# A decode-attention stream: one load cut into 128, 122 and 6 rows, and the last V tiles in fewer loads

## The chip, the core and the metric

The kernel runs on one core of one Trainium2 chip. Its metric is the device time of one launch in microseconds, the median of several runs. A profiled execution of the same program gives, beside its own time, the span from the core's first to its last instruction; every time of an instruction below counts from the start of that span.

## What is computed

One token attends to two caches, and a gate mixes both results. Part A has 16 heads with a cache each; part B has 16 query heads on 8 caches, two to a cache. All caches are 8192 x 256 in float32.

```
def _A_ref(x, k_cache, v_cache, wq, wo):          # H = 16, Dh = 256; B: Hq = 16 on Hkv = 8
    q = (x @ wq).reshape(B, Sq, H, Dh)            # x is 1 x 1 x 448
    scores = jnp.einsum("bhqd,bhkd->bhqk", q, k_cache) * (Dh ** -0.5)
    p = _softmax(scores, axis=-1)
    o = jnp.einsum("bhqk,bhkd->bhqd", p, v_cache)
    return o.reshape(B, Sq, H * Dh) @ wo          # 448 outputs
...
g = _sigmoid((x * gate_w).sum(-1, keepdims=True))
return g * a + (1 - g) * b
```

Each cache element is used for one or two query heads, so nearly all of the 432 MB that the core reads is K and V, read once.

## The kernel before

**One stream.** The host lays everything that is read (x and the gate's weights, Wq, K, V, Wo) into one flat array, in the order of use, and the core reads it from its start to its end. All loads are issued by SyncE on one queue. A buffer (a "slot") has 128 partitions of 15,872 floats (and 16 more), and there are three of them; `plan()` (line 47) cuts the stream into 54 fills of a slot. Most fills are one DMA of 128 rows, one row a partition, 62 KB a row (7936 KB). Within the array a DMA's rows lie one behind the other (line 469).

**Units and tiles.** There are 24 units (8 sets of one head pair of B, r = 2, and two heads of A, r = 0 and 1), each of four tiles of 2048 keys; a K tile or a V tile is 128 x 4096 floats, 2 MB. V runs three tiles behind K (`LEAD`). Each set's Wq stands ahead of its K, its Wo behind.

**The work on a piece** (`piece`, line 416) follows its load in the same order. For K, units with r = 2 and r = 1 take their scores on TensorE (`scores`, line 244, matmul on line 255); those with r = 0 take them on VectorE by row (`scores_by_row`, lines 277 and 281). Minimum, exponential and a transpose follow on VectorE and ScalarE. For V, `attend` (line 307) multiplies by the probabilities on TensorE, 16 rows of 128 keys to a tile, two rows to a matmul. After a unit's last V tile, `take` (lines 316 and 317) and `project_o` (line 372) bring the output into shape; small steps between (`combine`, `column`) are put off by one or two tiles with `wait` and `tick`.

**The order on TensorE** is the program's order: an instruction of a later piece waits behind one of an earlier piece.

**The end.** The last three fills are cut into smaller DMAs so that work can start before a fill is whole: 3072 and 4864 KB; 1280, 2048 and 2048 KB; and the last V tile as `LAST_CUT` = 8, 4 and 4 of its 16 rows (1024, 512 and 512 KB) with the last Wo in four DMAs (448, 448, 672 and 224 KB). In all there are 63 loads. Behind them stand the last `take` and `project_o`, the output matmuls (`emit`, line 398) in two batches of 32, a copy to SBUF (line 483) and the output's DMA, which has four rows of 448 bytes (line 484).

**Waits of the queue.** A fill is issued when its slot's last reader of three fills before is done. Beside that each DMA uses one of eight completion semaphores in turn, so that a load also waits for the landing of the eighth before it.

Of the kernel before, what the change touches and what calls it, by code (L numbers as in the profile page):

```python
# [14 lines left out]
P = 128  # L15
# [19 lines left out]
WQ = (4 * KF + 2) * DH  # L35
UNITS = [2, 0, 1]
BY_ROW = {(s, 0) for s in range(NS)}
LAST_CUT = [8, 4, 4]
HEAD_AT = {2: 0, 0: 2, 1: 3}
TILES = [((s, r), t) for s in range(NS) for r in UNITS for t in range(NT)]  # L40

# [5 lines left out]
def plan():  # L47

    size = {"xg": XG, "k": ROWS * DH, "v": ROWS * DH, "wq": WQ, "wo": 8 * D}
    per = len(UNITS) * NT  # L50
    n = len(TILES)
    items = []
    for i in range(n + LEAD):
        if i == 0:
            items += [("xg", 0), ("wq", 0)]
        if i < n:
            items.append(("k", i))
        if i >= LEAD:
            items.append(("v", i - LEAD))
        if i % per == 7 and i // per + 1 < NS:  # L60
            items.append(("wq", i // per + 1))
        if i % per == LEAD + 1 and i >= per:
            items.append(("wo", i // per - 1))
    loads, room = [[]], FULL
    last = [("v", n - 3), ("v", n - 2)]
    for kind, i in items[:items.index(last[0])]:
        at, left = 0, size[kind]
        while left:
            step = min(left, room) // ATOM[kind] * ATOM[kind]
            if step:  # L70
                loads[-1].append((kind, i, at, step))
            at, left, room = at + step, left - step, room - step * (kind != "xg")
            if left:
                loads.append([])
                room = FULL

    loads = [[x] for x in loads]
    x = loads[-2][0]
    loads[-2] = [x[:2], x[2:]]
    loads[-1] += [[(kind, i, 0, size[kind])] for kind, i in last]  # L80
    at, end = 0, []
    for c in LAST_CUT:
        end.append([("v", n - 1, at, c * DH)])
        at += c * DH

    for h, e, n in ((3, 0, 2), (0, 0, 2), (1, 0, 3), (2, 1, 1)):
        end.append([("wo", NS - 1, (2 * h + e) * D, n * D)])
    return loads + [end]


LOADS = plan()


@with_exitstack
def kernel(
# [5 lines left out]
    nc = tc.nc  # L101
# [314 lines left out]
    def piece(kind, i, at, view):  # L416
        n = view.shape[-1] // ATOM[kind]
        j0 = at // ATOM[kind]
        if kind == "xg":
            inputs(view[:, :KF + 1])  # L420
            GW[0] = view[:, KF + 1:]
        elif kind == "wq":
            project(i, j0, view.rearrange("p (c n) -> p c n", c=n))
            if j0 + n < 2 * KF + 1:
                pass
            elif i == 0:
                spread(0)
                prepare(GW[0])
            else:
                wait(1, spread, i)  # L430
        elif kind == "k":
            u, t = TILES[i]
            if u in BY_ROW:
                scores_by_row(u, t, 2 * j0, view.rearrange("p (j d) -> p j d", d=DH))
            else:
                scores(u, t, j0, view.rearrange("p (c n) -> p c n", c=n))
            if j0 + n < 2 * NG:
                return
            tick()
            if t == NT - 1:  # L440
                gather(u)
                wait(1, combine, u)
                wait(2, column, u)
        elif kind == "v":
            u, t = TILES[i]
            n = view.shape[-1] // DH
            attend(u, t, at // DH, n, view.rearrange("p (j d) -> p j d", d=DH))
            if at // DH + n == ROWS:
                if t == NT - 1:
                    take(u)  # L450
                    if u != TILES[-1][0]:
                        wait(1, project_o, u)
                if i >= len(TILES) - LEAD:
                    tick()
        elif kind == "wo" and i < NS - 1:
            emit_set(i, j0, view.rearrange("p (c n) -> p c n", c=n))
            if i == NS - 2 and j0 + n == 8:
                fold()
        else:
            for j in range(n):  # L460
                LAST[divmod(j0 + j, 2)] = view[:, j * D:(j + 1) * D]

    off = 0
    for fill in LOADS:
        buf = ring.tile([P, FULL + XG], F32, name="slot")
        c = 0
        for load in fill:
            n = sum(x[3] for x in load)
            nc.sync.dma_start(buf[:, c:c + n], stream[off:off + P * n].rearrange("(p n) -> p n", p=P))
            off += P * n  # L470
            for x in load:
                piece(*x[:3], buf[:, c:c + x[3]])
                c += x[3]
# [78 lines left out]
```

## Time and profile before

| | us |
|---|---|
| median of 3 runs | 1010.64 (1010.57 to 1010.64) |
| the profiled execution, its own time | 1010.95 |
| its span | 1009.2 |

| engine | busy us | share of the span |
|---|---|---|
| TensorE matmuls (PE) | 578.0 | 57% |
| VectorE (DVE) | 465.1 | 46% |
| ScalarE (ACT) | 90.0 | 9% |
| DMA queue q1, of 16 engines | | 99.1% |

Mean granted TensorE clock: 0.773 of full speed. The busy share of the DMA engines is a mean over the core's 16 engines. In lines with "out<-in", the first name is what is written; "x16" counts instructions; "[6.31 <-DMA slot]" is idle time before a group and what ended it.

### The profile page before, as it was taken

How to read it: one execution, taken by the hardware profiler on the slowest of the kernel's cores; microseconds unless marked ns; L12 is line 12 of the kernel's file. 1: busy time of each engine (PE TensorE's matmuls, PEld its weight loads, DVE VectorE, ACT ScalarE, POOL GpSimd, SP SyncE). 2: the span in 40 equal slices, each digit the busy share in tenths (PEclk: the TensorE clock that was granted, in tenths of full speed). 3: DMA queues.
4: the chain of work that ended last, by engine and by line, in shares of the span. 5: the costliest groups of instructions: out<-in, count | busy, mean ns of one | idle time of the engine just before them, and what ended most of it. 6: DMA issues, size and time to landing. Idle time of an engine off the chain costs nothing.

```text
span 1009.2 us, 7624 instructions
## 1 busy us (share of the span) xinstructions
PE 578.0 (57%) x3154; PEld 169.8 (17%) x3154; DVE 465.1 (46%) x732; ACT 90.0 (9%) x267; POOL 1.9 (0%) x10
## 2 busy tenths in 40 slices
PE   0846745565745655636646556645656537537557
PEld 0211211121211111112111111111211112111112
DVE  1486213961248521576215841248521585216851
ACT  0100100010100110001100001100110000101010
POOL 0000000000000000000000000000000000000000
PEclk9977877767777887867787777776886777777788
DMA  9999999999999999999999999999999999999997
GB/s 403 439 438 425 431 436 439 435 421 433 439 436 425 436 431 441 431 428 433 441 428 429 438 431 433 435 431 438 431 431 426 440 438 426 428 433 441 424 421 299
DMA packets 9114, 432.50 MB, mean 429 GB/s; under 512 B 1016, under 2 KB 1144, under 8 KB 1784
## 3 DMA queue, kind: packets, MB, share of 16 engines
q1 hardware_dynamic: 9080, 432.02, 99.1%
q8 instruction: 24, 0.39, 0.2%
q14 instruction: 10, 0.08, 0.0%
HBM read 432.02 MB, written 0.00 MB: 428 GB/s over the span
## 4 chain that ended last, share of the span: by engine, by line
DMA 71%; PE 14%; DVE 12%; ACT 2%; issue 1%; ACTq 0%; SPq 0%; DVEq 0%
DMA slot<-in_stream_dram 71%; PE o L307 6%; PE sc L255 5%; DVE sr L281 4%; DVE slot L277 4%; PE sm L220 2%; ACT px L264 1%; DVE mn L261 1%; DVE pr L267 1%; PE sm L237 0%; DVE pr L294 0%; ACT pxr L290 0%; ACT ew L345 0%; PE sm L361 0%; DVE st L262 0%
## 5 line engine op out<-in xcount | busy, mean ns | idle before, releaser
L307 PE MATMUL o<-slot,pr 128*32 128x512 f32 (+1 forms) x1536 | 349.9, 758 | 224.6 <-DMA slot<-in_stream_dram 224.6
L255 PE MATMUL sc<-slot,qb 128*32 128x512 f32 x1024 | 197.5, 715 | 104.7 <-DMA slot<-in_stream_dram 101.7
L261 DVE TENSOR_REDUCE mn<-sc 128x1 f32<-128x512 f32 x64 | 44.1, 690 | 325.7 <-PE sc L255 300.9
L277 DVE TENSOR_TENSOR slot<-slot,qa 128x4096 f32<-128x4096 f32 (+7 forms) x40 | 142.6, 3565 | 41.1 <-DMA slot<-in_stream_dram 41.0
L307 PEld LDWEIGHTS o<-slot,pr 128*32 128x32 f32 (+1 forms) x1536 | 80.0, 142 | 405.2 <-DMA slot<-in_stream_dram 252.8
L281 DVE TENSOR_REDUCE sr<-slot 128x16 f32<-128x4096 f32 (+7 forms) x40 | 142.7, 3567 | 1.4
L255 PEld LDWEIGHTS sc<-slot,qb 128*32 128x32 f32 x1024 | 46.3, 129 | 221.1 <-issue 126.1
L264 ACT ACTIVATE px<-sc,st 128x512 f32<-128x512 f32 x64 | 44.0, 687 | 408.5 <-DVE st L262 386.6
L267 DVE STREAM_TRANSPOSE pr<-px 128x512 f32<-128x512 f32 x64 | 45.6, 713 | 58.9 <-ACT px L264 58.9
L220 PE MATMUL sm<-slot,xz 128*32 128x512 f32 x128 | 45.7, 707 | 35.8 <-DVE xz L193 23.0
L290 ACT ACTIVATE pxr<-sr,st 128x16 f32<-128x16 f32 x32 | 9.8, 308 | 373.6 <-DVE st L288 373.6
L372 PE MATMUL sm<-sel,ob 128*128 128x1 f32 (+1 forms) x96 | 17.5, 287 | 37.3 <-DVE ob L317 37.3
L317 DVE SCALAR_TENSOR_TENSOR ob<-o,half,ob 128x256 f32<-128x256 f32 x24 | 11.3, 470 | 44.0 <-ACT ob L316 44.0
L372 PEld LDWEIGHTS sm<-sel,ob 128*128 128x128 f32 x96 | 15.5, 228 | 61.8 <-DVE ob L317 53.6
L220 PEld LDWEIGHTS sm<-slot,xz 128*32 128x32 f32 x128 | 11.1, 128 | 65.4 <-issue 27.8
L294 DVE TENSOR_TENSOR pr<-pxr,cols 128x256 f32<-128x256 f32 x32 | 13.6, 426 | 15.9 <-ACT pxr L290 15.9
L316 ACT ACTIVATE ob<-o,half 128x256 f32<-128x256 f32 x24 | 11.3, 469 | 49.5 <-PE o L307 49.5
L361 PE MATMUL sm<-ones,wr 1*128 1x1 f32 x48 | 9.7, 268 | 10.4 <-DVE wr L354 10.4
L237 PE MATMUL sm<-px,spread 64*128 64x256 f32 x16 | 6.6, 498 | 13.9 <-DVE es L347 13.9
L381 PE MATMUL Y<-slot,ocs 128*1 128x448 f32 x112 | 13.4, 595 | 0.0
L361 PEld LDWEIGHTS sm<-ones,wr 1*128 1x128 f32 x48 | 7.8, 203 | 32.8 <-issue 28.1
L264 ACT ACTIVATION_READ_ACCUMULATOR px<-sc,st 128x1 f32 x64 | 12.3, 193 | 0.0
(73 smaller groups left out, 142.4 us busy)
## 6 DMA issues: line engine op xcount, KB each, us to landing
slot<-in_stream_dram SPq DMA_DIRECT2D x50, 7936.0 KB, 42.6
slot<-in_stream_dram SPq DMA_DIRECT2D x1, 7940.0 KB, 22.0
slot<-in_stream_dram SPq DMA_DIRECT2D x1, 4864.0 KB, 41.0
slot<-in_stream_dram SPq DMA_DIRECT2D x2, 2048.0 KB, 25.3
slot<-in_stream_dram SPq DMA_DIRECT2D x1, 3072.0 KB, 29.9
slot<-in_stream_dram SPq DMA_DIRECT2D x1, 1280.0 KB, 20.8
slot<-in_stream_dram SPq DMA_DIRECT2D x1, 1024.0 KB, 24.2
slot<-in_stream_dram SPq DMA_DIRECT2D x2, 512.0 KB, 25.5
```

The source lines that it names most:

```text
L220: nc.tensor.matmul(q[BLK * a:BLK * (a + 1), :], xz[:, c if c < KF else KF + a, :], w[:, j, :], start=(c == 0), stop=(c == KF), skip_group_ ...
L255: nc.tensor.matmul(sc[32 * g:32 * (g + 1), :], qb[:, e, at:at + 32], kt[:, j, :], start=(e == 0), stop=(e == 1), skip_group_check=True)
L261: nc.vector.tensor_reduce(mn, sc, axis=AX.X, op=OP.min)
L264: nc.scalar.activation(px, sc, AF.Exp, bias=st[:, 0, t:t + 1], scale=-1.0, accum_out=st[:, 1, t:t + 1])
L267: nc.vector.transpose(pr.rearrange("p (q r k) -> p q k r", r=BLK, k=2), px.rearrange("p (q k c) -> p q k c", c=BLK, k=2))
L277: nc.vector.tensor_tensor(kt, kt, QA[u][:, None, :].to_broadcast([P, n, DH]), op=OP.mult)
L281: nc.vector.tensor_reduce(sc[:, j0:j0 + n], kt, axis=AX.X, op=OP.add)
L294: nc.vector.tensor_tensor(pr, px[:, :, None, :].to_broadcast([P, ROWS // 2, NG * NT, 2]), cols[:, t].rearrange("p g r -> p (g r)")[:, None ...
L307: nc.tensor.matmul(O[u][w * g:w * (g + 1), :], pr[:, j // 2, :w], vt[:, j - j0:j - j0 + 2, :], start=(t == 0 and j < 2 * P // w), stop=(t ...
L361: nc.tensor.matmul(cl, WR.pop(u).rearrange("p c x m k -> p (c x m k)"), ones[:1, :], start=True, stop=True)
L372: nc.tensor.matmul(oc[:, e, :M], OB[u][:, e::2], SEL[u][:, :M], start=True, stop=True)
L381: nc.tensor.matmul(YY[0][32 * h:32 * h + 1, :], OC[s, r][:, e, m:m + 1], wt[:, j, :], start=False, stop=(s == NS - 2 and e == 1), skip_gro ...
```

## The change

The second fill (the fill with number 1) goes as three DMAs: its 128 rows without their last 512 columns, then these 512 columns (2 KB a row) of rows 0 to 121 as one DMA and of rows 122 to 127 as another. Where the bytes go is unchanged. At the end, the fill of 3072 + 4864 KB is one DMA of 7936 KB; the piece of 1280 KB and the whole tile behind it go as one of 3328 KB; the last V tile is cut in 8 and 8 rows. There are 62 loads.

```diff
@@ -35,7 +35,10 @@
-LAST_CUT = [8, 4, 4]
+SKEW = 1
+SKEW_ROWS = 122
+SKEW_N = 512
+LAST_CUT = [8, 8]
@@ -75,9 +78,9 @@
     loads = [[x] for x in loads]
-    x = loads[-2][0]
-    loads[-2] = [x[:2], x[2:]]
-    loads[-1] += [[(kind, i, 0, size[kind])] for kind, i in last]
+    v1, v2 = [(kind, i, 0, size[kind]) for kind, i in last]
+    loads[-1][0].append(v1)
+    loads[-1].append([v2])
@@ -461,12 +464,17 @@
-    for fill in LOADS:
+    for f, fill in enumerate(LOADS):
         buf = ring.tile([P, FULL + XG], F32, name="slot")
         c = 0
         for load in fill:
             n = sum(x[3] for x in load)
-            nc.sync.dma_start(buf[:, c:c + n], stream[off:off + P * n].rearrange("(p n) -> p n", p=P))
+            rows = stream[off:off + P * n].rearrange("(p n) -> p n", p=P)
+            parts = [(0, P, 0, n)]
+            if f == SKEW:
+                parts = [(0, P, 0, n - SKEW_N), (0, SKEW_ROWS, n - SKEW_N, n), (SKEW_ROWS, P, n - SKEW_N, n)]
+            for p0, p1, n0, n1 in parts:
+                nc.sync.dma_start(buf[p0:p1, c + n0:c + n1], rows[p0:p1, n0:n1])
             off += P * n
```

## Rows read from the trace of the kernel before

**Rows 1.** The page: DMA engines' busy tenths in 40 slices of the span.

```profile
DMA  9999999999999999999999999999999999999997
```

**Rows 2.** The page: the chain that ended last, shares of the span by engine.

```profile
DMA 71%; PE 14%; DVE 12%; ACT 2%; issue 1%; ACTq 0%; SPq 0%; DVEq 0%
```

**Rows 3.** The chain of waits, its end: start us, us, what.

```profile
985.98 18.74 DMA slot<-in_stream_dram
...
1004.76 1.58 PE Y L398 x32
...
1006.37 0.27 DVE ys L483
```

**Rows 4.** Windows: us, busy of PE, PEld, DVE, ACT, POOL, PEclk, DMA share, GB/s.

```profile
920.00:960.00 40.00, 20.94 (x89) 6.03 (x89) 32.82 (x32) 2.52 (x10) 0.00 (x0) 0.75 1.00 433
...
996.00:998.00 2.00, 2.00 (x18) 0.55 (x10) 0.00 (x0) 0.00 (x0) 0.00 (x0) 1.00 1.00 405
998.00:999.00 1.00, 0.73 (x9) 0.16 (x8) 0.16 (x1) 0.00 (x0) 0.00 (x0) 1.00 0.99 396
999.00:1000.00 1.00, 0.78 (x6) 0.14 (x4) 0.00 (x0) 0.00 (x0) 0.00 (x0) 1.00 0.77 305
1000.00:1001.00 1.00, 0.80 (x6) 0.14 (x4) 0.00 (x0) 0.00 (x0) 0.00 (x0) 1.00 0.64 252
1001.00:1002.00 1.00, 0.91 (x4) 0.00 (x0) 0.00 (x0) 0.00 (x0) 0.00 (x0) 1.00 0.60 237
1002.00:1003.00 1.00, 0.00 (x0) 0.00 (x0) 0.48 (x1) 0.47 (x1) 0.00 (x0) 1.00 0.55 224
1003.00:1004.00 1.00, 0.94 (x20) 0.90 (x24) 0.17 (x2) 0.00 (x0) 0.00 (x0) 1.00 0.48 186
1004.00:1005.00 1.00, 0.81 (x36) 0.54 (x32) 0.00 (x0) 0.00 (x0) 0.00 (x0) 0.97 0.12 45
```

**Rows 5.** The page: DMA queue, kind: packets, MB, share of 16 engines.

```profile
q1 hardware_dynamic: 9080, 432.02, 99.1%
q8 instruction: 24, 0.39, 0.2%
q14 instruction: 10, 0.08, 0.0%
```

**Rows 6.** DMA packets of the window 1006:1009.2, which holds the output's DMA alone.

```profile
DMA packets 8, 0.00 MB, mean 1 GB/s; under 512 B 8, under 2 KB 8, under 8 KB 8
```

**Rows 7.** The page: DMA issues, KB each, us from issue to landing.

```profile
slot<-in_stream_dram SPq DMA_DIRECT2D x50, 7936.0 KB, 42.6
```

**Rows 8.** Waits of SyncE's DMA queue: us in total, times, longest.

```profile
SPq L469 <- DVE sr L281: 478.3, 24, 25.7
SPq L469 <- PE o L307: 158.2, 15, 16.6
SPq L469 <- DMA slot<-in_stream_dram: 152.5, 25, 10.9
```

**Rows 9.** Timeline of the end, some matmul groups: start us, us, instruction, count.

```profile
974.72 1.90 PE L255 MATMUL sc<-slot,qb 128*32 128x512 f32 x16
...
982.93 3.64 PE L307 MATMUL o<-slot,pr 128*32 128x512 f32 x16 [6.31 <-DMA slot<-in_stream_dram]
...
995.82 1.92 PE L307 MATMUL o<-slot,pr 128*32 128x512 f32 x16 [2.65 <-DMA slot<-in_stream_dram]
...
998.32 1.06 PE L307 MATMUL o<-slot,pr 128*32 128x512 f32 x8 [0.27 <-DMA slot<-in_stream_dram]
...
1000.86 1.05 PE L307 MATMUL o<-slot,pr 128*32 128x512 f32 x4 [0.20 <-DMA slot<-in_stream_dram]
...
1003.62 0.95 PE L398 MATMUL Y<-slot,ocs 128*1 128x112 f32 x32
...
1004.76 1.55 PE L398 MATMUL Y<-slot,ocs 128*1 128x112 f32 x32 [0.19 <-DMA slot<-in_stream_dram]
```

**Rows 10.** Windows of PE alone: us, busy of PE, PEclk, DMA share, GB/s.

```profile
982.90:989.00 6.10, 6.07 (x33) 0.59 1.01 429
```

## The prediction

> **What bounds the kernel now.** I read the slices of the DMA engines first: they are busy at 9 tenths or more in all slices but the last [rows 1]. The chain that ended last is DMA for 71% of the span [rows 2]; its other parts are work that released a slot while older loads still ran. So the transfers bound it: 432.02 MB on sixteen engines that are busy 99.1% of the span [rows 5]. The question is then whether an engine ever runs dry. SyncE does wait for readers of a slot, 478.3 and 158.2 us in all [rows 8], but a load of 7936 KB takes 7936 KB / 433 GB/s = 18.8 us [rows 4] and lands 42.6 us after its issue [rows 7]: some 23.8 us of older transfers lie ahead of each load when it is issued. The engines don't run dry, and a share of 1.00 from 920 to 960 us says the same [rows 4].
>
> The windows of the last microseconds then show what sets the end [rows 4]. All sixteen engines are busy up to 999 us; the share falls to 0.64 and 0.60 by 1002, stands at 0.55 from 1002 to 1003 and ends at 0.12. A share of 0.56 is nine of sixteen: some seven engines finish near 999 to 1000.5, the nine others at 1003 to 1004.8. Each of those nine still runs at full speed (224 GB/s over 8.8 engines is 25.5 a piece). Each DMA of 128 rows gives each engine eight rows, so the shares of data were equal, and the late engines lost their 4 to 5 us by something else. 34 instruction packets [rows 5] are the candidate. The chain ends with the last loads until 1004.72, 32 output matmuls of 1.58 us and the copy [rows 3].
>
> **What the change does, part by part.** The sum is made against the profiled execution, span 1009.2 and own time 1010.95, which is 0.31 above the median of 1010.64; I subtract from that median in the end.
>
> *Bytes of the second load.* The last 512 columns are 2 KB a row. At 433 GB/s / 16 = 27.1 GB/s an engine needs 0.0757 us for 2 KB [rows 4], so an engine that now moves eight such rows spends 0.605 us on them. Small rows cost more: from 996 to 998 us, with rows of 3.5 to 4 KB, all engines are busy but move 405 GB/s [rows 4]; 3.9 KB then takes 0.154 instead of 0.144 us, 0.010 us for each row, so 2 KB takes 0.086. Where the 128 pieces land decides all. The number of engines of a DMA is not always sixteen: 9080 packets [rows 5] are 63 x (128 + 16) + 8, one completion for each engine of a load, and the output's four rows made 8 packets [rows 6], four rows and four completions, so four engines. For 122 rows this trace has no case. The bounds: spread as now, 0; taken off most engines and put on few, -0.6 us for those relieved, and for a busy one, if two share 122 rows, 61 rows and one of the six: 62 x 0.086 - 0.605 = +4.7 us. (One engine alone would be given 128 x 0.086 - 0.6 = +10.4; I keep that as the far end and give it almost nothing.) I take the concentrated case on engines of the early lot, -0.6 for the end: the only row count here that isn't 128 used fewer than sixteen engines.
>
> [...]
>
> *Does the early lot have the room?* An early engine ends at about 999.5, so it would end at 999.5 + 4.7 = 1004.2, against 1004.8 - 0.6 = 1004.2 for the last of the late ones. It just fits. What covers the extra transfer is the idle 5 us at the end, nowhere else; the engine runs 4.7 us behind from the second load on, and loads 2 and later land up to that much later. The readers then free slots later, still within the 23.8 us of queued work [rows 7]; if that cover were gone the queue would idle by the difference.
>
> *Two more issues at the start, one fewer in all.* The added issues stand on SyncE before the third load, which has two loads, 37.6 us of transfers, ahead of it: nothing. The turn of the eight semaphores shifts by two, and each load then waits for an older landing; such waits are 152.5 us in 25 cases now [rows 8], all under queued transfers, and stay so.
>
> *Three fewer loads at the end.* Each engine handles 24 fewer rows of the small-row kind: 24 x 0.010 = 0.24 us less on all engines, ahead of the last V rows. [...]
>
> *Later work on TensorE.* The K tile whose scores ran at 974.72 now lands with the whole fill, where TensorE's wait ended at 982.93 less 0.8, near 982. So these scores, 16 matmuls in 1.90 us at full clock [rows 9], and the half V tile ahead of it, 8 of some 1 us, move behind 982. [...]
>
> *Coarser last cut.* Eight rows take 1.06 us, four took 1.05 [rows 9]: +0.01. The last V rows land where they did, and from there to the first batch of output matmuls the gap stays; this batch ends 0.19 us before the load that the second batch waits for [rows 9], so a delay over 0.2 us counts in full. The second batch took 1.55 against 0.95 us for the first [rows 9], so the clock fell within it; other idle times ahead may bring 0.6 either way. I take 0, as in the row.
>
> Sum: -0.6 - 0.24 + 0.01 = -0.83: own time 1010.95 - 0.8 = 1010.1, and median 1010.64 - 0.8 = 1009.8; with 0.05 for what the fit of the early lot may cost, 1009.9.
>
> **The rivals.**
>
> *R1, a busy engine is a late one (slower).* One mechanism: if 122 rows go to two engines and one of these is among the nine late ones, that one ends the run. Price +4.7 - 0.24 = +4.5, less that engine's own lead over the last. The nine end on average (0.48 + 0.12) x 16 / 9 = 1.1 us after 1003, 0.7 before the last [rows 4]: +3.8, 1014.4 (1013.7 to 1015.1). It decides as soon as the engine's lead is under about 4 us. For it: nine of sixteen are late, and no row names them. [...]
>
> *R2, nothing is concentrated (the skew doesn't take place).* 122 rows spread over sixteen engines: only the fewer small rows are left, -0.24: 1010.4.
>
> [...]
>
> *R4, all sixteen end together.* The engine time idle from 998 to 1005 is 0.01 + 0.23 + 0.36 + 0.40 + 0.45 + 0.52 + 0.88 = 2.85 us [rows 4], so no shift of bytes can gain more than 2.9 + 0.24: 1007.5 to 1008.5. Two engines alone can't level nine; nearly excluded.
>
> **How the numbers follow.** That few engines take the 122 rows I hold at 0.65 to 0.7, and that these are early ones at 0.6, a judgement and the weakest step here. Forecast 0.39; R1 0.27; R2 0.25; R3 0.06; R4 0.03. The forecast's own range is 1009.2 to 1010.5. The whole reaches from 1009.2, through R2 and R3, to the middle of R1: 1014.4; what is left out is R4 and half of R1, some 0.17. A difference of 0.2%, 2 us, is about what a measurement of this kernel can tell from none. Faster by more: R4 alone, 0.04. Within: the forecast, R2 and R3, 0.68. Slower: R1 and a little else, 0.28.
>
> **What would show it.** Packets on q1: sixty loads of 144, the output's 8 and the six rows' 12 give 8660; with 122 + 2 for the skewed DMA 8784, with 122 + 16 it is 8798. If the early lot took the bytes, the windows of the last 5 us stand at a share nearer to 0.7 than to 0.55 until the end, and the last load lands near 1003.9 in the span. If R1 holds, a long stretch at 0.06 or 0.12 stands at the end. If TensorE is late, the second half of the last V tile shows no wait for its load. The forecast is wrong if the span's end moves by over 2 us either way.

## The result, and the profile after

The changed kernel takes 1014.34 us (median of five, 1013.71 to 1014.93), the kernel before 1010.57 (1010.53 to 1010.64) on the same chip: a ratio of 1.0036, 95% interval 1.0025 to 1.0047. That is 3.8 us slower, where I forecast 0.7 us faster and gave "slower" 0.28. The profiled execution has its own time 1013.84 and its span 1012.1, both 2.9 us above those of before, so the traces can account for 2.9 of the 3.8.

The page first, each line for itself: DMA tenths in 40 slices, the queues' packets, the shares of the chain.

```profile
DMA  9999999999999999999999999999999999999996
...
q1 hardware_dynamic: 8784, 432.02, 99.0%
...
DMA 74%; PE 12%; DVE 12%; ACT 1%; issue 1%; SPq 0%; ACTq 0%; DVEq 0%
```

Against [rows 1, 2, 5] nothing large has changed: transfers bound it still, and DMA's part of the chain grew by three points. The count of packets is exact and answers the first open question: 8784 is the figure for 122 rows on two engines (and 6 rows on six).

The end of the chain (start us, us, what) shows where the 2.9 us stand.

```profile
979.61 28.52 DMA slot<-in_stream_dram
...
1008.17 0.99 PE Y L401 x32
...
1009.19 0.28 DVE ys L491
```

The tail of TensorE's timeline (the same columns; in brackets the idle time before) stands beside [rows 9].

```profile
986.48 1.94 PE L310 MATMUL o<-slot,pr 128*32 128x512 f32 x8 [8.73 <-DMA slot<-in_stream_dram]
988.19 3.64 PE L258 MATMUL sc<-slot,qb 128*32 128x512 f32 x16
...
1001.78 1.06 PE L310 MATMUL o<-slot,pr 128*32 128x512 f32 x8
1004.25 1.07 PE L310 MATMUL o<-slot,pr 128*32 128x512 f32 x8 [1.40 <-DMA slot<-in_stream_dram]
...
1007.05 0.95 PE L401 MATMUL Y<-slot,ocs 128*1 128x112 f32 x32
1008.17 0.95 PE L401 MATMUL Y<-slot,ocs 128*1 128x112 f32 x32 [0.17 <-DMA slot<-in_stream_dram]
```

Against [rows 3]: the last load but one (672 KB) releases the last output matmuls at 1008.17 instead of 1004.76, 3.41 us later; these take 0.99 instead of 1.58; the copy starts 2.82 later. So the last transfers are late by 3.4 us, and TensorE gives 0.6 back. TensorE itself isn't the bound: the second half of the last V tile still waited 1.40 us for its load.

Windows of the last microseconds (us, busy of PE, PEld, DVE, ACT, POOL, PEclk, DMA share, GB/s) tell who is late.

```profile
1003.00:1004.00 1.00, 0.00 (x0) 0.00 (x0) 0.00 (x0) 0.00 (x0) 0.00 (x0) 1.00 0.71 287
1004.00:1005.00 1.00, 0.75 (x8) 0.16 (x8) 0.00 (x0) 0.00 (x0) 0.00 (x0) 1.00 0.66 262
1005.00:1006.00 1.00, 0.31 (x4) 0.00 (x0) 0.05 (x1) 0.47 (x1) 0.00 (x0) 1.00 0.27 104
1006.00:1007.00 1.00, 0.51 (x4) 0.51 (x4) 0.43 (x1) 0.00 (x0) 0.00 (x0) 1.00 0.08 32
1007.00:1008.00 1.00, 1.00 (x34) 0.69 (x33) 0.16 (x1) 0.00 (x0) 0.00 (x0) 1.00 0.06 25
1008.00:1009.00 1.00, 0.83 (x32) 0.60 (x32) 0.00 (x0) 0.00 (x0) 0.00 (x0) 1.00 0.01 5
```

Up to 1005 the share is 0.66 to 0.71, eleven engines of sixteen where [rows 4] had nine: two early engines have joined the late ones, as forecast. But then 0.08 and 0.06 stand for two microseconds: 1/16 is 0.0625, so *one* engine runs alone, at 25 GB/s, about what each of the nine has in [rows 4] (224 GB/s over 0.55 x 16 = 8.8 engines, 25.5). It sets the end.

The records of the last load's sixteen completions, sorted, say it by engine (us after the first of them; the first itself in the second column):

```
kernel              first    the other fifteen
before              999.58   0.0 0.1 0.1 0.7 0.7 | 1.9 | 4.5 4.6 4.7 4.7 4.8 4.9 5.1 5.6 5.7
after              1000.82   0.1 0.1 0.7 1.0 | 4.6 4.6 4.6 4.7 4.8 5.0 5.1 5.3 5.5 5.9 | 7.9
```

Two engines left the early lot: one that stood near 0, and the one at 1.9. The completions of every load, read in turn, show how. When the third fill's load lands, two engines stand 5.4 and 5.6 us behind the first, where before the last of all was 1.5 behind. One of the two is still 5.3 behind at the end; the other loses another 1.0, 0.7 and 0.7 on the way and is the one at 7.9. And the first engine itself is 1.24 later, though it was to be relieved.

The same reading shows when the nine engines of the kernel before fell behind: at the instruction packets, which the prediction named as a candidate. From one load to the next the distances between the engines hardly move (their sum by 0.4 us at most), except around such a packet. Around one of 16 KB a single engine falls back by about 1.55 us (from 1.16 to 2.72 between the loads at 115 and 134 us, with a packet at 127.7), around one of 8 KB by 0.7 to 1.0. With 24 and 10 of them [rows 5], the sum of the sixteen distances grows from 5.3 us at the second load to 48.1 at the last.

### The profile page after: what moved, and what is told of

The parts are those of the page before. It is cut to its first block, busy times and chain, and to the rows that moved or that the text cites. A ratio compares the mean times of both kernels' runs of the same rounds, so it can differ in the third digit from the quotient of the medians.

```text
span 1012.1 us, 7626 instructions
## 1 busy us (share of the span) xinstructions
PE 576.6 (57%) x3154; PEld 168.1 (17%) x3154; DVE 465.0 (46%) x732; ACT 90.2 (9%) x267; POOL 1.9 (0%) x10
## 3 DMA queue, kind: packets, MB, share of 16 engines
q1 hardware_dynamic: 8784, 432.02, 99.0%
## 4 chain that ended last, share of the span: by engine, by line
DMA 74%; PE 12%; DVE 12%; ACT 1%; issue 1%; SPq 0%; ACTq 0%; DVEq 0%
DMA slot<-in_stream_dram 74%; PE o L310 6%; PE sc L258 5%; DVE sr L284 5%; DVE slot L280 5%; ACT px L267 1%; DVE mn L264 1%; DVE pr L270 0%; PE sm L223 0%; ACT ew L348 0%; SPq L477 0%; DVE pr L297 0%; ACT pxr L293 0%; PE sm L364 0%; PE sm L240 0%
## 5 line engine op out<-in xcount | busy, mean ns | idle before, releaser
L310 PE MATMUL o<-slot,pr 128*32 128x512 f32 (+1 forms) x1536 | 346.4, 747 | 228.1 <-DMA slot<-in_stream_dram 227.9
L258 PE MATMUL sc<-slot,qb 128*32 128x512 f32 x1024 | 202.9, 734 | 106.0 <-DMA slot<-in_stream_dram 105.8
```

The source lines that it names most:

```text
L258: nc.tensor.matmul(sc[32 * g:32 * (g + 1), :], qb[:, e, at:at + 32], kt[:, j, :], start=(e == 0), stop=(e == 1), skip_group_check=True)
L310: nc.tensor.matmul(O[u][w * g:w * (g + 1), :], pr[:, j // 2, :w], vt[:, j - j0:j - j0 + 2, :], start=(t == 0 and j < 2 * P // w), stop=(t ...
```

## The experiments

Medians in us; "before" is the kernel before on the same chip; the interval is that of the ratio.

| run | this | before | ratio, 95% |
|---|---|---|---|
| skew_only | 1013.93 | 1010.69 | 1.0030, 1.0018 to 1.0041 |
| tail_only | 1011.88 | 1010.69 | 1.0008, 0.9999 to 1.0017 |
| split16 | 1011.49 | 1010.69 | 1.0007, 0.9999 to 1.0016 |
| probe (one run) | 1018.13 | 1010.69 | |
| tail_merge | 1010.71 | 1010.64 | 1.0002, 0.9993 to 1.0011 |
| tail_cut | 1011.39 | 1010.64 | 1.0008, 0.9999 to 1.0017 |
| skew_dense | 1013.70 | 1010.64 | 1.0029, 1.0018 to 1.0041 |
| skew_big | 1018.11 | 1010.64 | 1.0072, 1.0059 to 1.0084 |
| skew_256 | 1011.14 | 1010.70 | 1.0004, 0.9995 to 1.0013 |
| rowshift | 1031.87 | 1010.70 | 1.0210, 1.0196 to 1.0224 |
| warm | 1010.57 | 1010.70 | 0.9998, 0.9989 to 1.0007 |
| split128 | 1010.82 | 1010.64 | 1.0001, 0.9992 to 1.0010 |

The ratio is an estimate of its own and needn't be the quotient of the two medians: for tail_only that would be 1.0012.

### Which half of the change costs?

*skew_only* is the kernel before with the second load cut as in the change:

```diff
+            rows = stream[off:off + P * n].rearrange("(p n) -> p n", p=P)
+            parts = [(0, P, 0, n)]
+            if f == 1:
+                parts = [(0, P, 0, n - 512)] + [(a, b, n - 512, n) for a, b in ((0, 122), (122, P))]
+            for p0, p1, n0, n1 in parts:
+                nc.sync.dma_start(buf[p0:p1, c + n0:c + n1], rows[p0:p1, n0:n1])
```

> The three DMAs of the second load with the old cut of the last loads. Theory: 1014.5, the whole of the loss and 0.2 more. Rival (the tail costs): near 1010 to 1011. In the trace the windows from 39 to 46 us should show whether all engines lose time there, some 2 us, or only those that hold the 122 rows.

*tail_only* is the changed kernel with the second load whole:

```diff
-            if f == SKEW:
+            if False:
```

> The second load as in the kernel before, only the last loads cut as in the changed kernel. If the skewed DMAs alone cost the 3.8 us (theory), this is at 1010.3, 0.2 below the kernel before, by 24 fewer small rows an engine. If the later K tile makes TensorE late at the end (rival), it is at 1011 to 1014 and the last V half has no wait for its load.

The skew alone costs 3.2 us. The tail alone costs 1.2 in the median, where a gain of 0.2 was expected, with an interval that just holds 1. The skew carries the result. The two would add to 4.4, not to 3.8; a possible reason stands under "The tail".

### Which engines are they?

*probe* adds, after fill 40, seven small DMAs of 1 to 7 rows, and a GpSimd memset of each one's tile, which has to wait for its landing; after fill 48 the same with 8 to 15 rows.

```diff
+        if f in (40, 48):
+            for k in range(1, 8) if f == 40 else range(8, 16):
+                pb = const.tile([16, 64], F32, name=f"pb{k}")
+                nc.sync.dma_start(pb[:k, :], stream[:k * 64].rearrange("(p n) -> p n", p=k))
+                nc.gpsimd.memset(pb[:k, :], 0.0)
```

No trace numbers the engines. In the expectations, here and below, engine 0 is the one that a DMA of one row runs on, engine 1 the one that a DMA of two rows has beside it, and so on. That each further row adds an engine to those before, and that the 122 rows ran on 0 and 1, is my assumption.

> The kernel before, with tiny DMAs of 1 to 7 rows behind fill 40 and of 8 to 15 rows behind fill 48; GpSimd overwrites each one's tile, so the start of its memset is the landing. If a DMA of k rows runs on the first k engines, the landing of k rows is that of the latest of these k. Theory: engine 0 early, and 1 early by 4 us or less, so that the start steps up by 1 to 2 us at two rows at most and by 3 to 5 us at some later count. Rival (engine 0 or 1 is of the nine late ones): the start at 1 or 2 rows is already 4 us behind the first engines. If the rows are spread in another way all starts agree. Its time is not of interest: some us over the kernel before.

The timeline of GpSimd in that run (start us, us, what, idle time before; the pause it puts into the stream makes the run 7.4 us slower):

```profile
771.23 0.14 POOL L478 MEMSET pb<- 1x64 f32 x1 [767.82 <-DMA pb<-in_stream_dram]
772.60 0.32 POOL L478 MEMSET pb<- 2x64 f32 x2 [1.23 <-DMA pb<-in_stream_dram]
776.17 0.68 POOL L478 MEMSET pb<- 4x64 f32 x4 [3.25 <-DMA pb<-in_stream_dram]
```

The DMA of one row is done at 771.23, those of two and three rows at 772.60, that of four at 776.17. The fifteen DMAs add 9320 - 9080 = 240 packets to q1, their 120 rows and 120 completions, as many as k engines for k rows give. The one-row DMA lands 0.18 us after the first completion of the load ahead of it (771.00), the two-row DMA 0.18 after one that is 1.38 behind that. I read each landing as that of the latest engine of its DMA: engine 0 is early, engine 1 is 1.4 us behind it, engine 2 no later than that, engine 3 some 5 us behind. If the 122 rows ran on engines 0 and 1, both are early ones, and engine 1 fits the lone 1.9 in the table of completions. That naming is assumed; the landings and the distances are measured. The table tells the same without names, since it is the early lot that lost two: R1's condition, that one of them is among the nine, doesn't hold. In the changed kernel the DMA of 122 rows has two completions, at 47.06 and 47.44 us, and that of 6 rows has six, four of them by 40.32 and two at 47.28 and 47.63, each some 0.2 behind one of the two, so I take the two busy engines to be among those six.

The eight memsets behind fill 48 run without a further wait from 930.04 on and order nothing. The first pause had let the engines draw level: at the next load the last is 1.9 us behind the first, not over 5 as ahead of the pause. An engine's lateness is thus gathered in the run and doesn't belong to the engine.

### How far does the cost follow the bytes?

*skew_256* moves 256 columns instead of 512 in the same way (122 and 6 rows).

```diff
+                parts = [(0, P, 0, n - 256)] + [(a, b, n - 256, n) for a, b in ((0, 122), (122, P))]
```

> As skew_only with 256 columns, 1 KB a row. Engine 1 then carries some 2.6 us more than the others instead of 5.3; with its own 2.0 it stays ahead of the late engines, so they set the end. If the others' loss goes with the bytes that two engines write alone, it is 1 us, less 0.3 us of relief: +0.7, 1011.4. If the others' loss goes with the number of short rows (61 an engine, as before) it stays at 2 us: 1012.4. If the loss came only from engine 1 ending last, there is none: 1010.4.

*skew_big* takes 1024 columns, as 64, 62 and 2 rows: an engine of the busy two gets 4 + 31 + 1 = 36 short rows, not 62, each twice as long. (q1 has 9228 packets, 80 + 64 + 4 more than before: sixteen, two and two engines. That the two are the same ones each time is assumed.)

```diff
+                parts = [(0, P, 0, n - 1024)] + [(a, b, n - 1024, n) for a, b in ((0, 64), (64, 126), (126, P))]
```

> The last 1024 columns of the second load as 64, 62 and 2 rows: engines 0 and 1 carry 28 rows of 4 KB more than in the kernel before, about the same bytes as 54 of 2 KB, in half as many pieces; the others have four rows of 4 KB less (the same 16 KB). If the others' loss goes with the number of short rows it halves to 1 us: 1012.5 to 1013. If it goes with the bytes or with the time that two engines work alone: 1013.9.

Half the bytes cost 0.4 us, within the interval; twice the bytes 7.5, more than either case of its expectation. So it isn't a price for each row: with 36 for 62 on the two engines skew_big costs more than twice as much.

*split128* cuts the second load in the same place but sends the 512 columns as one DMA of 128 rows; *split16* sends them as 112 and 16 rows, each DMA on sixteen engines (q1 has 9240 packets, (112 + 16) + (16 + 16) more than before).

```diff
+                parts = [(0, P, 0, n - 512), (0, P, n - 512, n)]                                                    # split128
+                parts = [(0, P, 0, n - 512)] + [(a, b, n - 512, n) for a, b in ((0, 112), (112, P))]                # split16
```

Theory A in the expectations assumes that a DMA of 128 rows pairs each engine with the same partitions every time; no trace names an engine or a partition.

> [...] If the pairing of engine and partition is what slows the engines (theory A), nothing is lost beyond the cost of eight more rows, 0.1 us: 1010.7, and the windows behind the second load are those of the kernel before. If short rows in the stream cost by themselves, some 0.5 us as in split16: 1011.2 or more.

> As skew_only, but the last 512 columns go as 112 and 16 rows, so that both counts divide by 16 and every engine has eight short rows as others have; same three DMAs, same bytes, same short rows. Theory (the concentration on two engines costs): 1010.7, the kernel before and 0.1 for eight more rows an engine. Rival (short rows or two more DMAs in the stream cost by themselves): 1012.6, with 2 us lost by all engines behind the second load.

split128 costs nothing, so 128 short rows and an additional DMA are free in this place. By the counts split16 has the same bytes on each engine as split128, and is 0.8 us above its before; the interval begins at 0.9999, but all eleven runs are at 1011.16 or more.

The trace records each DMA packet with its start and duration. From 15 to 90 us these records give the duration of a piece, in ns, mean and median:

```
kernel       short rows           62-KB rows begun 38:42  42:46  46:50 (means)
before       none                              2346   2362   2360
split128     2 KB:  84,  84                    2338   2362   2358
split16      2 KB:  99,  84                    2779   2372   2372
skew_256     1 KB:  60,  61                    2778   2494   2366
skew_dense   2 KB: 122, 132                    3122   3098   2445
after        2 KB: 121, 131                    2933   3119   2462
skew_big     4 KB: 292, 294                    4175   4074   3314
```

This is the centre of the case. In a DMA of 128 rows a 2-KB piece takes 84 ns, as the prediction's 0.086 says; with 122 and 6 rows it takes 121 in the mean (131 in the median). And the other engines' own rows, of the next loads, take up to 3.4 us instead of 2.34 while the short rows run. Windows show the same (columns as above). First the kernel before:

```profile
39.00:46.00 7.00, 4.43 (x22) 1.16 (x24) 3.01 (x6) 1.44 (x5) 0.00 (x0) 0.76 1.01 437
46.00:60.00 14.00, 6.51 (x30) 1.82 (x26) 11.98 (x18) 1.11 (x6) 0.00 (x0) 0.86 1.00 432
...
20.00:60.00 40.00, 25.77 (x131) 7.29 (x131) 18.32 (x37) 5.07 (x15) 0.00 (x0) 0.91 1.00 432
```

The kernel after:

```profile
39.00:46.00 7.00, 4.68 (x34) 1.52 (x32) 3.79 (x9) 2.09 (x6) 0.00 (x0) 1.00 1.15 372
46.00:60.00 14.00, 4.71 (x22) 1.18 (x18) 11.19 (x17) 0.82 (x4) 0.00 (x0) 0.76 0.93 397
...
20.00:60.00 40.00, 24.31 (x131) 7.06 (x131) 18.32 (x37) 5.07 (x15) 0.00 (x0) 0.91 0.99 402
```

And skew_big:

```profile
20.00:60.00 40.00, 24.72 (x131) 6.99 (x131) 18.31 (x37) 5.07 (x15) 0.00 (x0) 0.88 0.99 372
```

The share stays near 1 on the whole while the GB/s fall: the engines are busy, and slow. Whole packets are put down to one window, sixteen of 62 KB at a time, so a short window can be off by some per cent. The clean measure is the completion of the last load's first engine: 999.58 before, 999.75 split128, 1000.08 split16, 1000.09 skew_256, 1001.07 skew_only, 1001.08 skew_dense, 1003.82 skew_big. The fourteen engines that were to gain from the skew lose from it, 1.5 us with 512 columns, 0.5 with 256, 4.2 with 1024.

### What slows the rows?

Three causes were open: the short rows' distance in DRAM (62 KB from one to the next), their being short, and theory A, that an engine writes to other partitions than in a DMA of 128 rows. *skew_dense* lays the 128 pieces one behind the other in the array and keeps the two DMAs:

```diff
+    (q, i, at, w) = loads[1][0][-1]
+    loads[1] = [loads[1][0][:-1] + [(q, i, at, w - 512)], [(q, i, at + w - 512, 512)]]
...
+            for p0, p1 in ((0, 122), (122, P)) if n == 512 else ((0, P),):
+                nc.sync.dma_start(buf[p0:p1, c:c + n], rows[p0:p1])
```

> As skew_only, but the host lays the 128 pieces of 2 KB one behind the other, so that the DMAs of 122 and 6 rows read an unbroken stretch and not 2 KB at every 62 KB. If the pitch of the source made the other engines lose 2 us, they lose little here and the run is near 1012 (engine 1's own 5 us are left: +1.3). If what counts is that two engines write single short rows to all partitions, it stays at 1013.9 and the windows from 20 to 60 us move as little as in skew_only.

3.1 us, as skew_only's 3.2, with the pieces at 122 ns in the mean. The short rows' distance in DRAM is not it.

*rowshift* sends the whole second load, rows of 62 KB, as DMAs of 112 and 16 rows. All sixteen engines take part (the packets are below), by that count with eight rows each as before, seven and one, and nothing is short; only how the rows are dealt out is changed.

```diff
+            for p0, p1 in ((0, 112), (112, P)) if f == 1 else ((0, P),):
+                nc.sync.dma_start(buf[p0:p1, c:c + n], rows[p0:p1])
```

> [...] If writing to partitions that otherwise belong to another engine is what slows all engines (theory A), this load takes 4 to 7 us longer: 1014 to 1018. If it is the work of two engines alone (theory B), it costs next to nothing: 1010.8.

It costs 21.2 us, more than the load itself takes (18.8) and than the 4 to 7 of theory A. Its windows (columns as above):

```profile
20.00:60.00 40.00, 13.65 (x83) 4.10 (x83) 5.49 (x17) 3.48 (x9) 0.00 (x0) 0.75 1.01 224
60.00:80.00 20.00, 11.99 (x48) 3.14 (x48) 12.46 (x19) 1.61 (x6) 0.00 (x0) 0.76 0.96 411
```

And its page's line of q1 (packets, MB, share):

```profile
q1 hardware_dynamic: 9096, 432.02, 99.1%
```

9096 is 62 x 144 + (112 + 16) + (16 + 16) + 8: both DMAs ran on sixteen engines. They stay busy at 224 GB/s, half the rate. In the packet records the 62-KB rows of the 112 take 2.9 to 4.8 us, 4.2 in the mean, instead of 2.34, those of the 16 rows up to 8.6. So neither short rows nor few engines are needed. What all slow cases share, and split128 and before don't, is that an engine's rows aren't the eight of a DMA of 128 rows. Whether it is the writes to SBUF that meet, or the reads of other rows in DRAM at the same time, rowshift doesn't separate.

Theory B, next to no cost, is out. Theory A had a fifth to a third of the 21.2 us, and that engines meet at the partitions they write was not shown. In rowshift the first sixteen of the 112 rows all take 3.9 to 4.5 us, so the slowing is there from the first rows. In the skew the fourteen engines had 0.6 us of relief forecast, and they lost 1.5. Both amounts stay open.

### The tail

*tail_cut* is the kernel before with only the coarser last cut; *tail_merge* is tail_only with the old cut.

```diff
-LAST_CUT = [8, 4, 4]
+LAST_CUT = [8, 8]       # tail_cut; tail_merge puts [8, 4, 4] back into tail_only
```

> Only the last cut changed to 8 and 8, everything else as before. Theory: 1011.5 to 1012, TensorE idle over 1 us before the last V half and the clock at 0.5 in the last microseconds of at least the profiled run or of most runs. Rival: 1010.7, as the kernel before.

> The merged fills near the end with the last V tile still cut 8, 4, 4; the second load as before. Theory (the coarse last cut lets TensorE idle 1.4 us ahead of the last half, its granted clock falls and the output matmuls run at the lower level): 1010.4, with the clock at 1.0 up to 1004 us. Rival (the merged fills, which move a K tile's work, upset the clock): near tail_only, 1011.5 to 1012.

tail_merge is the kernel before (+0.07 us): fewer loads bring nothing that can be measured. tail_cut's runs reach from 1010.46 to 1012.75, tail_merge's from 1010.25 to 1011.78, before's from 1010.26 to 1011.24. By their intervals none differs from before; the median and the spread point to the cut, but don't secure it. The traces show what can happen. TensorE's timeline in tail_only:

```profile
998.25 1.07 PE L310 MATMUL o<-slot,pr 128*32 128x512 f32 x8 [0.21 <-DMA slot<-in_stream_dram]
1000.73 1.83 PE L310 MATMUL o<-slot,pr 128*32 128x512 f32 x8 [1.42 <-DMA slot<-in_stream_dram]
1003.71 1.01 PE L375 MATMUL sm<-sel,ob 128*128 128x1 f32 x4 [1.15 <-DVE ob L320]
1004.65 3.17 PE L401 MATMUL Y<-slot,ocs 128*1 128x112 f32 x64
```

Windows of the same run (columns as above):

```profile
1000.00:1002.00 2.00, 1.27 (x8) 0.16 (x8) 0.00 (x0) 0.00 (x0) 0.00 (x0) 0.72 0.61 240
1002.00:1004.00 2.00, 0.85 (x6) 0.29 (x2) 0.48 (x1) 0.47 (x1) 0.00 (x0) 0.50 0.49 194
```

TensorE's timeline in tail_merge:

```profile
1000.85 1.05 PE L310 MATMUL o<-slot,pr 128*32 128x512 f32 x4 [0.17 <-DMA slot<-in_stream_dram]
1003.06 0.63 PE L375 MATMUL sm<-sel,ob 128*128 128x1 f32 x4 [1.16 <-DVE ob L320]
1003.62 0.95 PE L401 MATMUL Y<-slot,ocs 128*1 128x112 f32 x32
1004.77 0.95 PE L401 MATMUL Y<-slot,ocs 128*1 128x112 f32 x32 [0.20 <-DMA slot<-in_stream_dram]
```

And in tail_cut:

```profile
1001.15 1.07 PE L307 MATMUL o<-slot,pr 128*32 128x512 f32 x8 [1.42 <-DMA slot<-in_stream_dram]
...
1005.06 1.64 PE L398 MATMUL Y<-slot,ocs 128*1 128x112 f32 x32 [0.17 <-DMA slot<-in_stream_dram]
```

With 8 and 8 rows TensorE idles 1.42 us ahead of the last half, with 8, 4 and 4 never over 0.3 ahead of a piece of that tile. In tail_only's profile the granted clock then fell, to 0.72 in the mean of 1000 to 1002 and 0.50 from 1002 on: the last V rows take 1.83 instead of 1.07, the 64 output matmuls 3.17. They end at 1007.82 instead of 1005.72, though the last transfer landed at 1005.15 against 1005.30. In tail_cut's profile, after the same 1.42, the clock was 1.00 until 1004, 0.79 in the mean of 1004 to 1006 and 0.50 behind that: the first batch took 0.95 us, the last 1.64. In the changed kernel it stayed at 1.00 to the end after an idle time of 1.40. From 996 to 1000 TensorE had been busy for 3.10 us in tail_only, 3.30 in tail_cut and all 4 in the changed kernel. So nearly the same idle time had three outcomes, and what decides among them stays open. In the changed kernel's profile the tail's cut cost nothing, which may be why the two halves don't add. The kernel before had a fall as well, in its last batch [rows 9], to a clock of 0.50 from 1005 to 1006.

*warm* puts 16 matmuls of zeros, which add nothing to the output, into the idle time ahead of the last `project_o` of tail_merge:

```diff
+    for _ in range(16):
+        nc.tensor.matmul(YY[0][:, :YN], zero, zero[:, :YN], start=False, stop=False, skip_group_check=True)
```

> tail_merge (last cut 8, 4, 4) with sixteen matmuls of zeros, 112 columns each, added to the output behind the last V matmuls, where TensorE waits 1.2 us for the last output to be brought into shape. If the clock at the end is what spreads the runs, more of them stay at the higher level and the median is 0.3 to 0.6 below tail_merge, 1010.2; if these matmuls are not enough to hold it, as tail_merge, 1010.7; if they delay the last product, 0.3 above.

1010.57 against 1010.70, no difference. No version here beats the kernel before.

## Why the prediction was wrong

**"Does the early lot have the room?" is the step that failed.** Concentration, two engines, both early: that much held. "An early engine ends at about 999.5 ... It just fits" gave both engines the lead of the first one, and a price of 4.7 us. The measured terms:

- *The price.* The piece was mis-sized, 0.086 us for 0.121 in the mean: 62 x 0.121 - 0.605 = +6.9, not +4.7. The row it came from [rows 4] was of 128-row DMAs, where 84 ns is right. The engine at 1.9 goes from 1001.5 to 1008.2 in skew_only (+6.7), to 1008.5 in skew_dense (+7.0) and to 1008.7 in the changed kernel (+7.2). The last is 0.5 above the sum less 0.24 for the merged loads; one of its instruction packets cost that engine 1.0 where the others cost 0.7. In skew_256 the same sum, 62 x 0.060 - 0.30 = +3.4, puts it at 1004.9, under the last one's 1005.7, and the time hardly moves.
- *The room.* That engine's lead over the last is 5.7 - 1.9 = 3.8 us, not 5.3 (the first engine's is 5.7). I read "some seven engines near 999 to 1000.5" off the shares as one lot; one of them wasn't. With the forecast's own price it would have ended 4.7 - 0.24 - 3.8 = 0.7 us after before's last one: no gain, and still no loss over 2 us. The price is the larger error: 7.2 for 4.7 - 0.24 = 4.5, so 2.7 us, against 5.3 - 3.8 = 1.5 of lead.
- Together: 7.2 - 3.8 = +3.4 at the last transfer, which is the +3.41 of the chain.

**"Bytes of the second load", the -0.6 for the relieved engines,** had the wrong sign: they lost 1.5 us (first completion +1.24 after -0.24 for the tail). It set nothing in the end, since one engine was later still; without the two the last would have landed at 1000.82 + 5.88 = 1006.7, 1.4 us after before's 1005.3, so the last transfer would have been later even with room to spare for the two. The step put all cost on the busy engines and none on those that work beside them.

**R1's number came out, not its mechanism.** 1014.4 was right for a late busy engine at +4.7; it was an early one at +7.2. That 1014.34 lies inside the whole range, just at its end, is luck. The sign that I named for R1, a long stretch at 0.06 or 0.12, thus can't tell the two; the table of completions can.

**What held.** The instruction packets, named as the candidate for the late engines, are where these fall back, by about 1.55 us at one of 16 KB. "Two more issues at the start": split128, with one more, shows no loss. "Later work on TensorE": its last half tile waited 1.40 us for the load. R3, which has 0.06 in the chances, is TensorE late at the end. No run shows the 1.2 us that I gave it: the 16 score matmuls at 988.19 did take 3.64 us, and the last half tile had its wait all the same.

**What isn't shown.** "Three fewer loads at the end", -0.24: the first engine ended 0.28 us earlier in tail_only, but 0.08 earlier in tail_merge with two loads fewer and 0.25 in tail_cut with one fewer, so the agreement says little. "Coarser last cut" was put at +0.01 with a clock of 0.6 either way; the lower clock cost 2.1 at the end of TensorE's work in tail_only's profile, and the medians have 0.7 to 1.2 that the intervals don't secure.

**Open:** why two engines slow the fourteen others by more than their bytes; what halves the rate in rowshift; in skew_big the sum 36 x 0.292 - 1.21 = +9.3 leaves 2.3 us of the last engine's 11.6 unexplained, part of which its slowed 62-KB rows can be.

## What to carry to other kernels

In this stream, bound by DMA, each other row count that was tried (122 and 6; 64, 62 and 2; 112 and 16) slowed rows: those of 62 KB begun from 38 to 42 us took 2.9, 4.2 and 2.8 us in the mean where 2.35 stood before, the last with 2-KB rows of 112 and 16. With the first two the slowing wasn't only on the engines that got more: the first completion of the last load came 1.5 and 4.2 us later. A price per piece therefore has to come from a DMA of the same shape. An average share of busy engines tells how many are early, not how early each is; before giving one more work, measure that one. And a coarser last cut that leaves TensorE idle near the end has to be priced with the lower clock as one case (3.17 us for 64 output matmuls in tail_only, 1.90 in tail_merge).

## What was unexpected of the hardware

- Eight 62-KB rows an engine cost 18.8 us in a DMA of 128 rows, and about twice that as seven and one, with the same engines and bytes: 224 instead of 432 GB/s from 20 to 60 us.
- 122 rows ran on two engines only (two completions, 8784 packets), and slowed rows on the fourteen others from 2.34 to as much as 3.4 us, although these moved less.
- The sixteen engines end up to 5.8 us apart with equal data, and in the same pattern in before, split128 and tail_merge: six within 0.8 us, one near 2, nine at 4.5 to 5.8. The distances grow in steps, one engine at a time, around the 34 instruction packets: about 1.55 us for one of 16 KB, though such a packet takes only 1.0 to 1.1 us itself.
